# Early-solve identity in fp32r, `u` kept in the masked-key tile, and a changed emission order behind the attention

## The chip, the cores and the metric

One core of one Trainium2 chip runs the whole program. The metric is the device time of one execution in microseconds (us). The profiler's span of an execution leaves out what lies around it; for the profiled execution of the kernel before, that is 1.84 us.

## The reference, cut to what matters

Three computations in a row, all float32 (some inputs are handed over as float64, and reach the kernel as pairs of 32-bit words). B = 4, H = 8, S = 768, D = 40; the two layers see 3072 tokens of 320 numbers.

```python
for t in range(S):                                   # linear attention with a state [B, H, D, D]
    y[:, :, t] = einsum('bhd,bhde->bhe', r_t, state)
    Sa = einsum('bhde,bhe->bhd', state, a_t)
    state = state * w_t[:, :, None, :] - Sa b_t^T + v_t k_t^T
x = y as [3072, 320]
h = x @ w_in;  x = (h * sigmoid(1.702 h)) @ w_out    # layer one, 2048 hidden numbers
g = x @ w_gate;  out = ((g * sigmoid(g)) * (x @ w_val)) @ w_out2    # layer two, 1536 hidden numbers
```

## The kernel before, in words

**Attention.** The sequence is cut into 12 chunks of 64 tokens. A chunk is a chain of small float32 products on PE with copies and elementwise work on DVE and ACT between them: scores (`nb`, L740; `nk`, L995), the inverse of a triangular matrix, `w` and `u` (L1067), the state `mt` (products `m_one` and `m_two`, L1098, and for early chunks L1107), and the output `y` (L1175). In the first five chunks (`EARLY`) the two halves of the inverse are joined on PE: `cross_mm` first writes an identity into the bank (L911, a 128x128 identity times a strip of 512 columns that repeats a 32-column identity, plain float32), and then adds the cross product (L917, `x`), which goes to ACT and back (L925 `join`).

**Layer one** (class Up). Six blocks `m` of 512 tokens times 16 parts `i` of the hidden size. `h_part` has 8 products L495 into the one bank `h`, then ACT silu (L503), ACT `gh` (L509), DVE `gl` (L510). Two parts later `o_part` has 8 products (L522 to L529) into the three banks of `sums`, which are three slices of one tile. After part 15 of a block the sums are evicted: L545 (ACT, bank 1), L548 (DVE, bank 0), then L555 (ACT) and L557 (DVE) on bank 2, each followed by a DMA into `x2s` from ACT's queue (L551, L559). The next block's first `o_part` waits for all of it. The weights `wo` of two parts come by four DMAs of SP (L485), into one of two tiles.

**Layer two** (class Down). Six blocks of 512 tokens times 12 parts `f`. `h_part` has 16 products (L1456), ACT silu (L1460), DVE product (L1461), ACT `gh` (L1462), DVE `gl` (L1463); `o_part` has 12 products (L1475 to L1477).

**Weights of layer two.** They arrive as float64 pairs and are converted in 351 small jobs for 45 pieces: SP load (L301), ACT mask (L307), DVE shift (L310), DVE join (L315), POOL add (L323), ACT high half (L1369), DVE low half (L1372); pieces of `gv_rest` are followed by copies between partitions (`wg` from `wg`, L1387, SP). `prepare(n, f)` issues the next `n` jobs in that fixed order, and more if part `f` still needs some. In layer one `prepare(11)` is called behind each `gl` of the dense tasks that are left once the attention has been issued (26 times); in layer two, block 0, `prepare(f=f)` ahead of each `h_part` and `prepare(8)` twice a part. `load_x` and `split_x` (L1430 to L1441) bring the next block's tokens.

**What sets the order.** In parts one and two a planner (class Plan) takes tasks with a cost, a due time, what they read and write, and the PSUM bank pair they need (three pairs: two `ps`, and the first two banks of `sums`), and writes each engine's order. Where it finds PE without work for too long it puts in placeholder products of zeros (`h<-still`, L453, function `warm`). Behind the attention's last task the dense tasks that are left (`tail`) are issued in program order by a loop in the main function. Engines run their own streams in order.

## Time and profile before

| | us |
| --- | --- |
| median of three timed runs | 1116.86 (1115.95 to 1124.56) |
| the profiled execution | 1112.34 |
| its span in the profile | 1110.5 |
| PE busy in the span | 1073.1 (97%) |
| DVE, ACT, POOL busy | 702.2, 436.0, 98.2 |
| first product of layer one | 125.5 |
| last `x2s` DMA of layer one issued, layer two alone behind it | 712.0 |

Read it as three stages. Up to 125.5 us there is attention only, with placeholders between its products. From there to about 592 us the planner interleaves attention and layer one; from 592 to 709 us layer one runs alone on PE while the weights of layer two are converted beside it; then comes layer two.

### The profile page before, as it was taken

How to read it: one execution, taken by the hardware profiler on the slowest of the kernel's cores; microseconds unless marked ns; L12 is line 12 of the kernel's file. 1: busy time of each engine (PE TensorE's matmuls, PEld its weight loads, DVE VectorE, ACT ScalarE, POOL GpSimd, SP SyncE). 2: the span in 40 equal slices, each digit the busy share in tenths (PEclk: the TensorE clock that was granted, in tenths of full speed). 3: DMA queues.
4: the chain of work that ended last, by engine and by line, in shares of the span. 5: the costliest groups of instructions: out<-in, count | busy, mean ns of one | idle time of the engine just before them, and what ended most of it. 6: DMA issues, size and time to landing. Idle time of an engine off the chain costs nothing.

```text
span 1110.5 us, 38519 instructions
## 1 busy us (share of the span) xinstructions
PE 1073.1 (97%) x16682; PEld 892.6 (80%) x16682; DVE 702.2 (63%) x1406; ACT 436.0 (39%) x814; POOL 98.2 (9%) x115
## 2 busy tenths in 40 slices
PE   8999999899999999999999999999999999999987
PEld 7777777678778787888788878888888888888876
DVE  8976797989697887979653667643443343443221
ACT  3443646454343534344343656432222222222221
POOL 0131123320100000000000323210000000000000
PEclk9896999999999999999999999999999999999999
DMA  6265547664353543544224677430423434341000
GB/s 209 73 184 171 180 150 219 180 195 140 113 166 111 161 133 103 162 127 137 87 62 131 201 212 228 142 90 1 141 69 115 124 116 126 96 147 59 24 1 27
DMA packets 141011, 141.88 MB, mean 128 GB/s; under 512 B 16032, under 2 KB 131744, under 8 KB 140832
## 3 DMA queue, kind: packets, MB, share of 16 engines
q1 hardware_dynamic: 134784, 131.48, 39.1%
q10 hardware_dynamic: 6048, 7.86, 2.1%
q8 instruction: 132, 2.16, 0.8%
q14 instruction: 47, 0.39, 0.1%
HBM read 118.04 MB, written 13.11 MB: 118 GB/s over the span
## 4 chain that ended last, share of the span: by engine, by line
PE 87%; DVE 5%; issue 3%; DMA 2%; ACT 1%; SPq 1%; ACTq 0%; POOL 0%; DVEq 0%
PE gv L1456 24%; PE h L495 15%; PE sums L527 4%; PE oacc L1477 4%; PE oacc L1476 4%; PE oacc L1475 4%; PE sums L528 3%; PE sums L529 3%; PE h L453 3%; PE ps L1175 2%; PE sums L523 2%; PE ps L1098 2%; PE sums L522 2%; PE ps L1227 2%; PE ps L740 1%
## 5 line engine op out<-in xcount | busy, mean ns | idle before, releaser
L1456 PE MATMUL gv<-xst,wg 128*128 128x512 f32 x1152 | 279.9, 395 | 0.0
L1456 PEld LDWEIGHTS gv<-xst,wg 128*128 128x128 f32 x1152 | 213.4, 188 | 45.7
L495 PE MATMUL h<-xst,wi 120*128 120x512 f32 x768 | 197.1, 398 | 0.0
L1461 DVE TENSOR_TENSOR sg<-gv,sg 128x512 f32<-128x512 f32 x72 | 49.8, 692 | 186.5 <-PE gv L1456 184.4
L495 PEld LDWEIGHTS h<-xst,wi 120*128 120x128 f32 x768 | 140.5, 188 | 30.6
L503 ACT ACTIVATE sg<-h 128x512 f32<-128x512 f32 x96 | 57.2, 596 | 152.6 <-PE h L495 145.0
L1462 ACT ACTIVATE gh<-sg 128x512 fp32r<-128x512 f32 x72 | 45.5, 632 | 143.0 <-DVE sg L1461 143.0
L510 DVE TENSOR_TENSOR gl<-sg,gh 128x512 fp32r<-128x512 f32 x90 | 63.4, 704 | 60.2 <-ACT gh L509 60.0
L1460 ACT ACTIVATE sg<-gv 128x512 f32<-128x512 f32 x72 | 43.0, 597 | 136.6 <-PE gv L1456 136.6
L323 POOL TENSOR_TENSOR cvw<-cvu,cva 128x256 uint32<-128x256 uint32 (+2 forms) x89 | 71.6, 805 | 274.1 <-DVE cvu L315 168.5
L1476 PE MATMUL oacc<-wo,gh 128*128 128x320 f32 x288 | 89.0, 309 | 0.0
L1477 PE MATMUL oacc<-wo,gl 128*128 128x320 f32 x288 | 89.0, 309 | 0.0
L1475 PE MATMUL oacc<-wo,gh 128*128 128x320 f32 x288 | 89.0, 309 | 0.0
L527 PE MATMUL sums<-gh,wo 128*128 128x512 f32 x192 | 80.8, 421 | 2.9 <-DVE sg L557 2.6
L1463 DVE TENSOR_TENSOR gl<-sg,gh 128x512 fp32r<-128x512 f32 x72 | 49.9, 692 | 50.2 <-ACT gh L1462 50.2
L528 PE MATMUL sums<-gh,wo 128*128 128x512 f32 x192 | 75.5, 393 | 0.0
L529 PE MATMUL sums<-gl,wo 128*128 128x512 f32 x192 | 75.2, 392 | 0.0
L509 ACT ACTIVATE gh<-sg 128x512 fp32r<-128x512 f32 x96 | 60.7, 632 | 3.6 <-ACT sg L503 0.3
L788 DVE TENSOR_TENSOR tsol<-tsol,tmp 128x126 f32<-128x126 f32 (+22 forms) x217 | 56.3, 260 | 6.7
L780 DVE TENSOR_TENSOR tmp<-tsol,nsol 128x126 f32<-128x126 f32 (+22 forms) x217 | 55.8, 257 | 6.9
L453 PE MATMUL h<-still 128*128 128x512 f32 x183 | 58.3, 466 | 1.1 <-DVE still L412 1.1
L1476 PEld LDWEIGHTS oacc<-wo,gh 128*128 128x128 f32 x288 | 54.1, 188 | 3.2
(182 smaller groups left out, 1618.8 us busy)
## 6 DMA issues: line engine op xcount, KB each, us to landing
wo<-w_out SPq DMA_DIRECT2D x192, 160.0 KB
cva<-out SPq DMA_DIRECT2D x128, 128.0 KB
cva<-gv SPq DMA_DIRECT2D x96, 128.0 KB
kb<-kba SPq DMA_DIRECT2D x92, 104.0 KB
cva<-in_ab SPq DMA_DIRECT2D x64, 120.0 KB
r<-rT SPq DMA_DIRECT2D x48, 104.0 KB
vt<-vT SPq DMA_DIRECT2D x48, 104.0 KB
a<-kba SPq DMA_DIRECT2D x46, 104.0 KB
```

Source lines behind the costliest of these rows:

```text
L323: nc.gpsimd.tensor_tensor(w.bitcast(U32), u, lo, op=ALU.add)
L453: self.nc.tensor.matmul(self.ph[0], c.to_broadcast([128, 128]), c.to_broadcast([128, 512]), start=True, stop=True)
L495: nc.tensor.matmul(ps[:, 0:n], self.wi[:, b, 128 * f:128 * f + 128], x[:, a], start=(e == 0), stop=(e == 7))
L509: add("ACT", 0.63, lambda: nc.scalar.activation(out=hi, in_=sg, func=ACTF.Copy), (f"sg{s}",), (f"gh{d}",))
L510: add(("DVE", "POOL"), (0.74, 1.35), lambda e: self.engine(e).tensor_tensor(lo, sg, hi.bitcast(F32), op=ALU.subtract), (f"sg{s}", f"gh{d}" ...
L527: nc.tensor.matmul(acc[k], w[:, c:c + 128], hi, start=st, stop=False)
L528: nc.tensor.matmul(acc[k], w[:, 256 + c:384 + c], hi, start=False, stop=False)
L529: nc.tensor.matmul(acc[k], w[:, c:c + 128], lo, start=False, stop=sp)
L1456: nc.tensor.matmul(ps, w[:, b], x[:, a], start=(i == 0), stop=(i == 7))
L1475: nc.tensor.matmul(acc[k], hi[:, c], self.wo[:, f, 0], start=st, stop=False)
L1476: nc.tensor.matmul(acc[k], hi[:, c], self.wo[:, f, 1], start=False, stop=False)
L1477: nc.tensor.matmul(acc[k], lo[:, c], self.wo[:, f, 0], start=False, stop=sp)
```

## The change

1. The identity strip of `cross_mm` comes from a new fp32r tile `ones`, filled by two POOL copies at the start, and the planner's numbers for that task are lowered (cost 2.7 to 1.8, work 2900 to 2600, size 261 to 259, real 2.5 to 1.6).
2. The tile `u` is gone: `u` is written into `nk`. So the next chunk's `nk` products come behind the products that read `u`.
3. `sums` has two banks and the third is a tile of its own, `third`. The first two banks are both evicted by ACT, the third by DVE in two steps, and the three `x2s` DMAs stand behind all of them.
4. In the tail, SP's tasks and the `x2s` DMAs are held back to just behind the next `gl` (and behind its `prepare`); `prepare(11)` is left out where an eviction stands before the next `gl`; `load_x(0)` comes 28 PE tasks before the end instead of 14.

```diff
-        self.sums = q.tile([128, 3, 512], F32, name="sums")
-        self.acc = [self.sums[:, i] for i in range(3)]
+        self.sums = q.tile([128, 2, 512], F32, name="sums")
+        self.acc = [self.sums[:, 0], self.sums[:, 1], q.tile([128, 512], F32, name="third")]
...
+            first = len(plan.tasks)
+            moves = []
             for k in range(2):
                 s = sg_slot()
                 t = self.sg[s]
-                if k:
-                    add("ACT", 0.6, lambda t=t: nc.scalar.activation(out=t, in_=acc[1], func=ACTF.Copy, scale=1 / 1.702),
-                        ("acc",), (f"sg{s}",))
-                else:
-                    add("DVE", 0.7, lambda t=t: nc.vector.tensor_scalar(
-                        out=t, in0=acc[0], scalar1=1 / 1.702, scalar2=None, op0=ALU.mult), ("acc",), (f"sg{s}",),
-                        port=False)
-                add("ACT", 0.4, lambda t=t, k=k: nc.scalar.dma_start(out=xs[128 * k:128 * k + 128], in_=t),
-                    (f"sg{s}",), (), kb=256)
+                add("ACT", 0.6, lambda t=t, k=k: nc.scalar.activation(out=t, in_=acc[k], func=ACTF.Copy, scale=1 / 1.702),
+                    ("acc",), (f"sg{s}",))
+                moves.append((xs[128 * k:128 * k + 128], t, s, 256))
             s = sg_slot()
             t = self.sg[s][0:64]
-            add("ACT", 0.6, lambda: nc.scalar.activation(out=t, in_=acc[2][64:128], func=ACTF.Copy, scale=1 / 1.702),
-                ("acc",), (f"sg{s}",))
+            add("DVE", 0.65, lambda: nc.vector.tensor_scalar(
+                out=t, in0=acc[2][64:128], scalar1=1 / 1.702, scalar2=None, op0=ALU.mult), ("acc",), (f"sg{s}",),
+                port=False)
             add("DVE", 0.72, lambda: nc.vector.scalar_tensor_tensor(
                 out=t, in0=acc[2][0:64], scalar=1 / 1.702, in1=t, op0=ALU.mult, op1=ALU.add), ("acc",), (f"sg{s}",), port=False)
-            add("ACT", 0.5, lambda: nc.scalar.dma_start(out=xs[256:320], in_=t), (f"sg{s}",), (), kb=128)
+            moves.append((xs[256:320], t, s, 128))
+            for o, t, s, kb in moves:
+                add("ACT", 0.4, lambda o=o, t=t: nc.scalar.dma_start(out=o, in_=t), (f"sg{s}",), (), kb=kb)
+            for t0 in plan.tasks[first:]:
+                t0.out = True
...
-        self.i32 = cst[:, C_I:C_I + 32]
+        self.ones = one.tile([128, 160], F32R, name="ones")
...
-        self.u = one.tile([128, 16, T], F32, name="u")
+        self.u = self.nk
...
-        nc.gpsimd.memset(self.u, 0.0)
+        nc.gpsimd.memset(self.nk, 0.0)
...
+        nc.gpsimd.tensor_copy(self.ones[:, 0:128], self.ident)
+        nc.gpsimd.tensor_copy(self.ones[:, 128:160], cst[:, C_I:C_I + 32])
...
-                    ps[:, 0], self.ident, self.i32.unsqueeze(1).to_broadcast([128, 16, 32]), start=True, stop=False,
+                    ps[:, 0], self.ones[:, 0:128], self.ones[:, 128:160].unsqueeze(1).to_broadcast([128, 16, 32]), start=True, stop=False,
...
-            plan.add("PE", 2.7, cross_mm, ("xa", "dd"), ("x.p",), due + 0.1, bank=bx, into=("q0", "q1"), work=2900,
-                     size=261, real=2.5)
+            plan.add("PE", 1.8, cross_mm, ("xa", "dd"), ("x.p",), due + 0.1, bank=bx, into=("q0", "q1"), work=2600,
+                     size=259, real=1.6)
...
-        middle = plan.add("PE", 1.25, u_mm, ("w",) + tt, ("u.p",), due + 0.01, bank=bu, into=("u",))
-        plan.add(("ACT",), (0.74,), u_out, ("u.p",), ("u",), due + 0.01, bank=bu)
+        middle = plan.add("PE", 1.25, u_mm, ("w",) + tt, ("u.p",), due + 0.01, bank=bu, into=("nk",))
+        plan.add(("ACT",), (0.74,), u_out, ("u.p",), ("nk",), due + 0.01, bank=bu)
...
-            plan.add("PE", 1.25, m_two, ("u", "tok1"), ("m.p",), due + 0.02, bank=bm, work=2200)
+            plan.add("PE", 1.25, m_two, ("nk", "tok1"), ("m.p",), due + 0.02, bank=bm, work=2200)
...
-        plan.add("PE", 0.9, ut_mm, ("u",), ("ut.p",), due + 0.03, bank=bx, into=("ut",))
+        plan.add("PE", 0.9, ut_mm, ("nk",), ("ut.p",), due + 0.03, bank=bx, into=("ut",))
...
-                    parts = iter(())
-                    for t in tail:
+                    parts, later = iter(()), []
+                    for i, t in enumerate(tail):
+                        if t.eng == "SP" or hasattr(t, "out") and t.kb:
+                            later.append(t)
+                            continue
                         if t.eng == "PE":
                             if left == 2:
                                 down.begin()
                             left -= 1
                         t.run()
                         if hasattr(t, "last"):
-                            down.prepare(11)
+                            ends = [hasattr(x, "last") for x in tail[i + 1:]] + [True]
+                            if not any(hasattr(x, "out") for x in tail[i + 1:i + 1 + ends.index(True)]):
+                                down.prepare(11)
+                            for x in later:
+                                x.run()
+                            later = []
                         if t.eng == "PE":
-                            if left == 14:
+                            if left == 28:
                                 down.load_x(0)
                             elif left == 10:
                                 parts = down.split_x(0)
                             next(parts, None)
+                    for x in later:
+                        x.run()
```

**PE, 15th part of layer one, fifth chunk.** Before: L522 and L495 are dense products, L965 is `t_mm`, L453 the placeholder, L740 the next chunk's scores.

```order
L522 MATMUL sums<-gh_100,wo_106 128x512
L495 MATMUL h<-xst_93,wi 128x512 x8
L965 MATMUL ps_123<-q,tn 32x32 x32
L453 MATMUL h<-still 128x512 x4
L740 MATMUL ps_122<-kb,a_126 32x32 x4
L740 MATMUL ps_122<-kb,a_126 32x64 x4
L740 MATMUL ps_122<-kb,a_126 32x32 x4
```

After (three lines further down in the file; L1051 is `w_two`, L1070 `u_mm`):

```order
L959 MATMUL ps_124<-tt,nb_141 32x32 x32
L495 MATMUL h<-xst_93,wi 128x512 x8
L1039 MATMUL ps_123<-v,nk 64x40 x32
L968 MATMUL ps_124<-q,tn 32x32 x32
L453 MATMUL h<-still 128x512
L1051 MATMUL ps_123<-mt,a_127 64x40 x32
L453 MATMUL h<-still 128x512 x7
L1070 MATMUL ps_124<-w,tt 64x40 x32
L1110 MATMUL ps_123<-mt,cst 104x320 x2
```

The scores of the next chunk (L740, L743 after) no longer stand ahead of `u_mm`, and one and seven placeholders stand there instead of four; five more follow behind L1085 of the same chunk. In all there are 194 placeholders instead of 183: 178 ahead of the first product of layer one before and 176 after, 5 behind it before and 18 after.

**ACT, the boundary between blocks 4 and 5 of layer one.** Before: L545 and L555 evict, L551 and L559 send, L503 and L509 belong to the first parts of block 5, L307 and L1369 are conversions.

```order
L1369 ACTIVATE wo_10357<-cvw_79 128x256
L307 ACTIVATE cva_76<-cva_76 128x256
L1369 ACTIVATE wg<-cvw_80 128x2x128
L545 ACTIVATE sg_98<-sums 128x512
L551 DMA x2s<-sg_98 128x512
L555 ACTIVATE sg_95<-sums 64x512
L551 DMA x2s<-sg_97 128x512
L503 ACTIVATE sg_96<-h 128x512
L509 ACTIVATE gh_100<-sg_96 128x512
L559 DMA x2s<-sg_95 64x512
L307 ACTIVATE cva_77<-cva_77 128x256
L1369 ACTIVATE wg<-cvw_79 128x2x128
```

After (L546 evicts, L558 sends, L1372 is the former L1369):

```order
L503 ACTIVATE sg_96<-h 128x512
L509 ACTIVATE gh_99<-sg_96 128x512
L546 ACTIVATE sg_97<-sums 128x512
L546 ACTIVATE sg_98<-sums 128x512
L503 ACTIVATE sg_96<-h 128x512
L509 ACTIVATE gh_100<-sg_96 128x512
L1372 ACTIVATE wg<-cvw_80 128x2x128
L307 ACTIVATE cva_77<-cva_77 128x256
L1372 ACTIVATE wg<-cvw_79 64x2x128
L558 DMA x2s<-sg_97 128x512
L558 DMA x2s<-sg_98 128x512
L558 DMA x2s<-sg_95 64x512
```

Both evictions stand together, no conversion stands ahead of them and none between `L509` and them, and the DMAs come behind the next part's L503 and L509 and three conversions.

**DVE, layer two, block 0, part 9 into part 10.** Before: L1461 and L1463 are the product and `gl` of a part, L1438 and L1441 split the next block's tokens.

```order
L1461 TENSOR_TENSOR sg_96<-gv,sg_96 128x512
L1463 TENSOR_TENSOR gl_102<-sg_96,gh_99 128x512
L1438 TENSOR_TENSOR xst_94<-xr,xst_94 128x512
L1461 TENSOR_TENSOR sg_97<-gv,sg_97 128x512
L1463 TENSOR_TENSOR gl_103<-sg_97,gh_100 128x512
L1441 SCALAR_TENSOR_TENSOR xst_94<-xst_94,cst,xr 128x512
```

After (L1464, L1466, L1441 and L1444 are the former L1461, L1463, L1438 and L1441, L1375 the former L1372):

```order
L1466 TENSOR_TENSOR gl_102<-sg_96,gh_99 128x512
L1441 TENSOR_TENSOR xst_94<-xr,xst_94 128x512
L1375 TENSOR_TENSOR wg<-cvw_79,wg 128x2x128
L310 TENSOR_SCALAR cvu_81<-cva_78 128x256
L315 SCALAR_TENSOR_TENSOR cvu_81<-cva_78,cvu_81 128x256
L1375 TENSOR_TENSOR wg<-cvw_80,wg 128x2x128
L310 TENSOR_SCALAR cvu_82<-cva_76 128x256
L315 SCALAR_TENSOR_TENSOR cvu_82<-cva_76,cvu_82 128x256
L1375 TENSOR_TENSOR wg<-cvw_79,wg 64x2x128 x2
L310 TENSOR_SCALAR cvu_81<-cva_77 128x256
L315 SCALAR_TENSOR_TENSOR cvu_81<-cva_77,cvu_81 128x256
L1375 TENSOR_TENSOR wo_10539<-cvw_80,wo_10539 128x256
```

Conversions now stand between part 9 and part 10, among them the last piece of `gv_rest` (L1375 on 64 partitions, twice). Before, the last conversion of all stood behind the `gl` of part 3. In the tail of layer one `prepare(11)` now runs 16 times (176 jobs) instead of 26 (286): the attention's last product stands behind part 75 of layer one and not part 67, and two calls are left out. So 175 jobs and not 65 are left to block 0 of layer two.

## Rows read from the trace of the kernel before

**Rows 1.** The page, the chain that ended last, share by engine.
```profile
PE 87%; DVE 5%; issue 3%; DMA 2%; ACT 1%; SPq 1%; ACTq 0%; POOL 0%; DVEq 0%
```
**Rows 2.** Windows: length, busy per engine PE PEld DVE ACT POOL, granted PE clock, DMA.
```profile
0.00:125.50 125.50, 113.40 (x3084) 91.35 (x3084) 101.44 (x166) 49.83 (x102) 21.00 (x32) 0.88 0.52 157
44.00:52.00 8.00, 7.85 (x167) 6.38 (x167) 7.42 (x19) 4.07 (x9) 0.66 (x1) 0.62 0.12 33
80.00:100.00 20.00, 17.56 (x472) 13.27 (x466) 12.21 (x27) 8.42 (x18) 2.94 (x4) 0.66 0.77 238
...
652.00:656.00 4.00, 4.00 (x18) 3.29 (x19) 2.86 (x6) 1.63 (x5) 1.10 (x2) 1.00 0.94 313
```
**Rows 3.** Timeline of PE, first chunk's solve: start, duration, line, count.
```profile
30.93 1.02 PE L911 MATMUL ps<-cst 128*128 128x512 f32 x2
32.03 1.25 PE L917 MATMUL ps<-nsol,tsol 32*16 32x32 f32 x128
33.21 2.45 PE L453 MATMUL h<-still 128*128 128x512 f32 x10
```
**Rows 4.** PE's waits, one group: total, times, longest (us).
```profile
PE sums L527 <- DVE sg L557: 2.6, 1, 2.6
```
**Rows 5.** Timeline around the boundary of blocks 4 and 5; in brackets the idle time before.
```profile
647.38 2.00 PE L495 MATMUL h<-xst,wi 120*128 120x512 f32 x8
...
649.25 0.58 ACT L545 ACTIVATE sg<-sums 128x512 f32<-128x512 f32 x1
...
649.86 0.69 DVE L548 TENSOR_SCALAR sg<-sums 128x512 f32<-128x512 f32 x1
...
651.21 0.68 DVE L557 SCALAR_TENSOR_TENSOR sg<-sums,sg 64x512 f32<-64x512 f32 x1 [0.66 <-ACT sg L555]
...
651.94 0.50 PE L527 MATMUL sums<-gh,wo 128*128 128x512 f32 x1 [2.56 <-DVE sg L557]
```
**Rows 6.** The same timeline at the boundary of layer one and layer two.
```profile
709.92 0.69 DVE L548 TENSOR_SCALAR sg<-sums 128x512 f32<-128x512 f32 x1 [2.12 <-ACT sg L545]
```
**Rows 7.** Timeline, layer two, block 0, parts 9 and 10 of before, PE and DVE.
```profile
751.23 3.89 PE L1456 MATMUL gv<-xst,wg 128*128 128x512 f32 x16
...
756.72 3.66 PE L1456 MATMUL gv<-xst,wg 128*128 128x512 f32 x15
...
756.62 0.69 DVE L1463 TENSOR_TENSOR gl<-sg,gh 128x512 fp32r<-128x512 f32 x1 [0.70 <-ACT gh L1462]
757.23 0.68 DVE L1438 TENSOR_TENSOR xst<-xr,xst 128x512 fp32r<-128x512 f32 x1
```
**Rows 8.** Timeline of the last conversions of before, each engine's step.
```profile
722.76 0.41 ACT L1369 ACTIVATE wg<-cvw 128x256 fp32r<-128x256 f32 x1
...
723.18 0.29 DVE L310 TENSOR_SCALAR cvu<-cva 128x256 uint32<-128x256 uint32 x1
723.50 0.42 DVE L315 SCALAR_TENSOR_TENSOR cvu<-cva,cvu 128x256 uint32<-128x256 uint32 x1
723.84 0.42 DVE L1372 TENSOR_TENSOR wg<-cvw,wg 128x256 fp32r<-128x256 f32 x1
...
724.14 0.75 POOL L323 TENSOR_TENSOR cvw<-cvu,cva 128x256 uint32<-128x256 uint32 x1 [2.36 <-DVE cvu L315]
...
728.70 2.72 SPq L1387 DMA_DIRECT2D wg<-wg  x4
```
**Rows 9.** Timeline, a small copy's issue on two queues and the work that waited for it.
```profile
593.51 2.28 SPq L1255 DMA_DIRECT2D xm<-su  x3
...
595.91 0.81 ACTq L1255 DMA_DIRECT2D xm<-su  x1
597.74 0.42 ACT L1262 ACTIVATE xst<-xm 120x256 fp32r<-120x256 f32 x1 [2.04 <-DMA xm<-su]
```
**Rows 10.** Timeline of SP's queue behind a part of layer one: loads for conversion, loads of `wo`.
```profile
645.19 2.90 SPq L301 DMA_DIRECT2D cva<-gv  x6
...
651.34 1.94 SPq L485 DMA_DIRECT2D wo<-w_out  x4
```

## The prediction

> **What bounds the kernel now.** I read the chain that ended last first: PE holds 87% of it [rows 1], and of 1110.5 us of span PE is busy 1073. So a microsecond counts if PE issues less, waits less, or runs at a higher clock; work on another engine counts only where PE waits for it. The windows come next. They show the one stretch where the clock is not full: 0.88 on average up to 125.5 us, with 0.62 at 44 to 52 and 0.66 at 80 to 100 [rows 2]. At a mean of 0.88 the stretch loses 0.12 x 125.5 = 15 us of full-speed time; the two dips hold 0.38 x 8 = 3.0 and 0.34 x 20 = 6.8 of it. Then PE's waits: with dense work there is a single long one, 2.6 us for an eviction [rows 4]. Last, the timelines at the three places that the change touches.
>
> **Identity.** The two records of L911 (the plain float32 product runs as two) start at 30.93 and L917 follows at 32.03 [rows 3]: a slot of 1.10 us, with PE waiting for nothing between. In the new type it is one pass of 512 columns. The trace has no 128x512 fp32r identity, but its dense products are of that type and width: 16 take 3.89 us and step by (756.72 - 751.23 - 12 x 0.147) / 16 = 0.233 [rows 7], so one alone lasts 3.89 - 15 x 0.233 = 0.40; with 0.08 for the change of type behind the drain I take 0.48 (my choice). That is -0.62 in each of five chunks, **-3.1**. Lower bound 0, if the cross product then waits for DVE anyway; upper bound -0.9 each where the clock is at half and the slot longer, -4.4.
>
> **Placeholders.** Eleven more, nearly all behind the first dense product. Ten take 2.45 us, a step of 0.24 [rows 3]: **+2.6** if PE had no gap there; 0 if they fill gaps that PE has anyway. I take the first, since from 125.5 on PE has next to no gap.
>
> **u in nk.** The order changes in the first chunk alone, where `nk_mm` of the next chunk goes behind `u`'s readers; in the later chunks it stood there already. It has placeholders on both sides there, which are the cover: 0. Without that cover, the scores of one chunk, 1.2 us, would move onto the chain.
>
> **Eviction.** Before, each of the four steps waits for the one before, on the other engine: 649.25, 649.86, 651.21 at the start of three of them, end 651.89, and PE resumes at 651.94 after 2.56 us [rows 5]. After, ACT does 0.58 + 0.6 while DVE does about 0.65 + 0.68, 1.35 us, and no conversion stands ahead of them on ACT. The block's last sum is issued just ahead of the eight products at 647.38, which take 2.00 [rows 5], so 1.35 is covered: **-2.56, +0.3** for what comes late behind (the silu of the fourth part waits for the `x2s` DMA that now stands behind three conversions; 0 to 2). What makes the four steps serial is the tile and not the bank: L548 stood idle 2.12 us until L545 was done, though it reads another bank [rows 6]. The Trainium skill, PSUM — Partial Sum Buffer, in its table of terms, says that two engines collide only on the same bank and the same quarter of the partitions; by that rule alone L548 could have run beside L545 before, and the split would be worth nothing. The trace speaks against that reading, so the split counts.
>
> **Conversions pushed into layer two.** This is the largest term. 176 jobs and not 286 are done in the tail, 175 are left at 16 a part, so by part 10 of block 0 336 are issued and 349 are wanted: 13 go directly ahead of `h_part(0,10)`, with the last `gv_rest` piece among them. Let t0 be the end of `h_part(0,9)`, 754.96 in before's time. `gl` is done at 757.31 (t0 + 2.35), the token split on DVE at 757.91 (+2.95) [rows 7]. Behind them on DVE: a low half 0.42, shift 0.29, join 0.42, with 0.03 between, at +4.1; POOL 0.75, +4.85; ACT 0.41, +5.3; issue of the copy 2.72 / 4 = 0.68, +5.95 [rows 8]; and its landing. For that I have an xst that waited for small copies: the last of SP's three is issued by 595.79, the one on ACT's queue by 596.72, and the work starts at 597.74 [rows 9], so 1.0 or 1.95 us. So the third product of part 10, which reads that piece, can go at +7.0 to +7.9. It is wanted at 12 x 0.147 + 2 x 0.233 = +2.23. The stall is 4.7 to 5.7; with up to 0.35 of backlog on DVE from the part before I take **+5.5** (0 if the pieces are ready, 8 if SP's queue is occupied). Queued behind it: PE's part 10 alone, and block 1 is not late for anything else. The other 160 jobs lie beside products: a part lasts 5.49 us on PE (756.72 - 751.23), and about two pieces ask DVE for 2 x (0.29 + 0.42 + 0.42) = 2.3 beside its own 2 x 0.69 + 0.68 = 2.1.
>
> **wo loads.** They are now issued behind one more part's `gl` and its conversion loads. A part of layer one is 16 x 0.23 = 3.68. From `gl` of one part (R): 3.68, six loads 2.9, one issue 1.94 / 4 = 0.49 [rows 10], landing 1.95: R + 9.0; the product that reads it stands five half parts on, R + 5 x 1.84 = 9.2. So it is just in time or, with a partition copy or a buffer wait in SP's queue, late by 0.3 to 0.8. In four pairs of parts: **+1.5** (0 to 5).
>
> **Early clock.** The order ahead of layer one has the same products, with more placeholders before the scores of chunk 2 (13, was 7) and before the solve's end in chunks 3 and 4, just ahead of the two dips. I give back a fifth of their 9.8 us: **-2** (from -10, both gone, to +7, a third dip of the size of the larger).
>
> **Sum.** -3.1 + 2.6 + 0 - 2.56 + 0.3 + 5.5 + 1.5 - 2 = +2.2 on 1112.34, so 1114.6 for an execution like the profiled one. The median of the timed runs is 4.5 above the profiled execution, so against 1116.86 this is **1119**.
>
> **Rivals.**
> *A, conversions keep up.* If the jobs run ahead of the order that I count (part 10 has no stall) and `wo` is in time, the sum is -3.1 + 2.6 - 2.3 - 2 = -4.8: 1112. For it: DVE is idle for most of layer two's parts in before. Against: the engines run in order, and the rows in DVE's stream stand behind part 9's `gl`.
> *B, the other side: the clock stays up.* If the order ahead of layer one keeps PE's clock full, the 15 us of the first stretch come back whole in place of 2: 1119 - 13 = 1106, and 1100 with A. It decides if both dips are gone, not one. For it: the dips follow stretches with little on PE, and the placeholders are denser now. Against: the number ahead of layer one hardly changes (178 and 176).
> *C, the gap costs the clock.* PE idles over 5 us in part 10, more than anywhere with dense work in before; the gap of 2.56 left the clock at 1.00 [rows 2]. If it falls for as long as at 44 to 52 us, another 3.0 us are lost, if as at 80 to 100, 6.8: 1122 to 1126. The Trainium skill, TensorE: Matmul & The Clock Gate, section HAM oscillation, says that idle gaps between bursts of products bring the clock to half and that each burst behind one starts cold. By that rule the gap in part 10 costs its stall and a cold start; the trace shows dips only in the first 125 us, and no gap of this length.
> *D, late wo at every pair.* If each of some ten pairs of the tail is late by 1 us and not four by 0.4, 8.5 more: 1128. It decides from 1.1 us a pair on.
> *E, the identity does nothing,* as DVE ends the chain there: +3.1, 1122.
>
> **How the numbers follow.** My case 0.45 (1115 to 1123 with its own bounds), A 0.22, B 0.08, C 0.12, D 0.08, E 0.05. A measurement of this kernel can tell about 1% from no change (11.2 us). Only B is below 1105.7, only the upper ends of C and D reach past 1128: faster 0.09, same 0.83, slower 0.08. The range leaves most of B and D out: 1108 to 1127.
>
> **What would show it.** In the profile of the changed kernel: one record of the identity of 0.4 to 0.5 us and L917 right behind; ACT's two evictions and DVE's two side by side, and PE's wait for them gone; a wait of about 5 us on PE at the third product of part 10 of layer two's first block, released by a copy `wg` from `wg`; short waits of PE for `wo` in the tail; the clock at 0.6 to 0.7 again in two places before the first dense product. Wrong would be: no wait in part 10 (A), a mean clock near 1.00 in the first stretch (B), a clock under 1.00 behind part 10 (C), or PE waiting for `wo` in most parts (D).

## The result, and the profile after

The changed kernel takes 1131.66 us in the median of six runs (1127.83 to 1136.7); the kernel before, run in turn with it, 1118.78 (1115.95 to 1124.56). The ratio is 1.0127, interval 1.0096 to 1.0158: slower by 13 us in the medians and 14 by the ratio, where the prediction had 1119 as the likeliest, 1108 to 1127 as its range and 0.08 for slower. A second set on another chip gives 1.0112 (1.0072 to 1.0151).

The profiled execution of the changed kernel took 1127.83 us, its span 1126.0, 15.5 more than that of the kernel before. The page shows less PE work and more waiting around it; in the chain PE has fallen from 87% [rows 1] to 78%, and DMA has risen from 2% to 5%:

```profile
PE 1072.2 (95%) x16688; PEld 890.9 (79%) x16688; DVE 699.9 (62%) x1400; ACT 435.0 (39%) x814; POOL 101.0 (9%) x123
...
PE 78%; DVE 7%; DMA 5%; issue 4%; SPq 2%; ACT 2%; POOL 0%; ACTq 0%; DVEq 0%; POOLq 0%
```

PE's waits by group (total, times, longest, in us) name what is new. The wait for the eviction [rows 4] is gone; one for the partition copy `wg` from `wg`, some for `wo`, and one for a silu stand instead:

```profile
PE gv L1459 <- DMA wg<-wg: 7.3, 1, 7.3
...
PE sums L527 <- DMA wo<-w_out: 2.3, 3, 1.4
...
PE h L495 <- ACT sg L503: 0.9, 1, 0.9
```

The windows, with the columns of [rows 2], show the first stretch at a granted clock of 0.99 (1.00 is full speed) in this execution, where it was 0.88, and half speed at another place, in part 10 of layer two's first block:

```profile
0.00:114.30 114.30, 100.59 (x3080) 82.74 (x3080) 98.30 (x160) 48.71 (x100) 22.76 (x32) 0.99 0.56 170
...
763.60:768.20 4.60, 0.61 (x3) 0.17 (x2) 3.87 (x9) 2.86 (x7) 1.02 (x2) 1.00 0.25 69
768.20:775.10 6.90, 3.60 (x9) 2.85 (x10) 3.48 (x8) 2.28 (x5) 2.12 (x3) 0.51 0.45 127
```

**Part 10.** PE's timeline (start, duration, line, count, idle time before) has its first two products, the wait, and the start of part 11:

```profile
763.58 0.63 PE L1459 MATMUL gv<-xst,wg 128*128 128x512 f32 x2
771.50 4.88 PE L1459 MATMUL gv<-xst,wg 128*128 128x512 f32 x13 [7.29 <-DMA wg<-wg]
...
778.21 1.33 PE L1459 MATMUL gv<-xst,wg 128*128 128x512 f32 x5
```

Part 10 takes 778.21 - 763.58 = 14.63 us where a part takes 5.49 [rows 7]: **9.1 us** more, of which 7.3 are the wait; the rest goes with the clock, 0.51 in the window from 768.2 on, in which PE works for 3.6 us. DVE, POOL and SP in the same stretch show why the copy is late:

```profile
760.83 0.74 POOL L323 TENSOR_TENSOR cvw<-cvu,cva 128x256 uint32<-128x256 uint32 x1 [3.02 <-DVE cvu L315]
...
760.87 0.86 DVE L310 TENSOR_SCALAR cvu<-cva 128x256 uint32<-128x256 uint32 x1
...
762.44 0.87 DVE L310 TENSOR_SCALAR cvu<-cva 128x256 uint32<-128x256 uint32 x1
...
763.69 0.68 DVE L1464 TENSOR_TENSOR sg<-gv,sg 128x512 f32<-128x512 f32 x1
...
765.07 0.69 DVE L1466 TENSOR_TENSOR gl<-sg,gh 128x512 fp32r<-128x512 f32 x1 [0.70 <-ACT gh L1465]
...
769.33 2.65 SPq L1390 DMA_DIRECT2D wg<-wg  x4
```

Measured from the end of part 9's products (761.82, counted as the prediction counted t0), the product L1464 starts at +1.87 where before it started at +0.27 (755.23 - 754.96), since conversions stand ahead of it on DVE; `gl` ends at +3.94 and not at +2.35, the copy is issued at +7.5, and PE resumes at +9.7 where it wanted +2.2. A shift L310 takes 0.86 and not 0.29 [rows 8] when it starts beside POOL's L323, and two pieces of a burst stand 762.44 - 760.87 = 1.57 us apart.

**The boundary of blocks 4 and 5.** The rows of ACT, DVE, ACT's queue, SP and PE that answer to [rows 5]:

```profile
650.86 1.08 ACT L546 ACTIVATE sg<-sums 128x512 f32<-128x512 f32 x2 [0.35 <-PE sums L529]
...
651.34 0.69 DVE L551 TENSOR_SCALAR sg<-third 64x512 f32<-64x512 f32 x1
...
652.07 0.68 DVE L554 SCALAR_TENSOR_TENSOR sg<-third,sg 64x512 f32<-64x512 f32 x1
...
653.61 0.50 PE L528 MATMUL sums<-gh,wo 128*128 128x512 f32 x1 [0.18 <-DMA wo<-w_out]
...
653.67 0.84 ACTq L558 DMA_DIRECT2D x2s<-sg  x2
...
659.41 0.60 ACT L503 ACTIVATE sg<-h 128x512 f32<-128x512 f32 x1 [4.28 <-DMA x2s<-sg]
...
659.58 2.18 SPq L485 DMA_DIRECT2D wo<-w_out  x4
...
660.06 2.11 PE L495 MATMUL h<-xst,wi 120*128 120x512 f32 x8 [0.89 <-ACT sg L503]
```

The eviction takes 652.75 - 650.86 = 1.9 us on two engines side by side, and the next `o_part` waits only for `wo`. But two things come late behind it. The `sg` tile that the first `x2s` DMA sends is the one that the silu at 659.41 writes next: that DMA is issued at 653.67 and lands at 659.33, ACT waits 4.28 us for it, and PE 0.89 us for the silu. And SP issues the next `wo` at 659.58, because its queue stood behind `load_x(0)`, which the change brought forward to this place. The view of the chain that ended last, from 648 to 664 us (start, us, what):

```profile
651.96 6.07 DMA xr<-x2s
...
658.09 0.68 SPq L1390
...
659.58 3.17 DMA wo<-w_out
...
662.80 0.50 PE sums L527
```

L1390 copies `wg` and doesn't read `xr`; in the trace it counts on the same semaphore as the first load of `load_x(0)`, and so waits for its landing. The three `x2s` DMAs beside that load take 5.5 to 7.3 us from issue to landing. Before, where `load_x(0)` was issued 29 us behind them, they took 2.0 to 3.9.

From the first product of part 84 (the parts of layer one counted from 1 to 96) to layer two the changed kernel needs 708.58 - 655.33 = 53.25 us, the kernel before 701.73 - 653.90 = 47.83, **5.4 us** less (these four are starts of rows of PE's timeline, of after and of before):

```profile
655.33 0.86 PE L495 MATMUL h<-xst,wi 120*128 120x512 f32 x3
...
708.58 0.62 PE L1459 MATMUL gv<-xst,wg 128*128 128x512 f32 x2
```
```profile
653.90 0.85 PE L495 MATMUL h<-xst,wi 120*128 120x512 f32 x3
...
701.73 0.62 PE L1456 MATMUL gv<-xst,wg 128*128 128x512 f32 x2
```

At 655.33 the changed kernel is 1.4 us late, at layer two 6.9, behind part 10 16.0. So the profiled difference is 1.4 up to and with the eviction, 5.4 in the tail and 9.1 in part 10. A part without a wait takes 3.68 us here; by the lengths of the parts from 84 on, 1.1 of the 5.4 go with the silu and 4.3 with late `wo`, the largest 1.2 in part 85 (662.80) and 1.9 in part 95.

**Ahead of the eviction.** The 1.4 hide a gain and a loss. The first product of layer one comes 125.5 - 114.3 = 11.2 us earlier in this execution, but part 83 starts 650.88 - 647.38 = 3.5 later. Windows from the first product of layer one to the attention's last, after and before:

```profile
114.30:625.10 510.80, 490.65 (x11246) 398.52 (x11241) 374.15 (x797) 222.37 (x395) 43.76 (x46) 0.99 0.45 136
```
```profile
125.50:592.10 466.60, 453.51 (x11105) 368.23 (x11102) 369.76 (x789) 211.69 (x376) 43.28 (x39) 1.00 0.47 142
```

PE is idle there for 20.2 us and not 13.1, and the clock is at half in three places, 13.6 us in sum.

### The profile page after: what moved, and what is told of

Same layout as the page of the kernel before. It is cut to its first block, busy times and chain, and to the rows that moved or that the text cites. A ratio compares the mean times of both kernels' runs of the same rounds, so it can differ in the third digit from the quotient of the medians.

```text
span 1126.0 us, 38515 instructions
## 1 busy us (share of the span) xinstructions
PE 1072.2 (95%) x16688; PEld 890.9 (79%) x16688; DVE 699.9 (62%) x1400; ACT 435.0 (39%) x814; POOL 101.0 (9%) x123
## 4 chain that ended last, share of the span: by engine, by line
PE 78%; DVE 7%; DMA 5%; issue 4%; SPq 2%; ACT 2%; POOL 0%; ACTq 0%; DVEq 0%; POOLq 0%
PE gv L1459 21%; PE h L495 14%; PE sums L527 4%; PE sums L528 3%; PE sums L529 3%; PE oacc L1480 3%; PE oacc L1478 3%; PE oacc L1479 3%; PE ps L1230 2%; PE third L523 2%; PE ps L1178 2%; PE third L522 2%; PE ps L1101 2%; DMA wo<-w_out 1%; PE h L453 1%
## 5 line engine op out<-in xcount | busy, mean ns | idle before, releaser
L495 PE MATMUL h<-xst,wi 120*128 120x512 f32 x768 | 197.4, 399 | 0.9 <-ACT sg L503 0.9
L495 PEld LDWEIGHTS h<-xst,wi 120*128 120x128 f32 x768 | 140.3, 188 | 32.0 <-ACT sg L503 1.5
L1464 DVE TENSOR_TENSOR sg<-gv,sg 128x512 f32<-128x512 f32 x72 | 49.8, 692 | 177.8 <-PE gv L1459 176.4
L503 ACT ACTIVATE sg<-h 128x512 f32<-128x512 f32 x96 | 57.2, 596 | 156.4 <-PE h L495 133.2
L323 POOL TENSOR_TENSOR cvw<-cvu,cva 128x256 uint32<-128x256 uint32 (+2 forms) x89 | 74.4, 836 | 272.3 <-DVE cvu L315 154.3
L1463 ACT ACTIVATE sg<-gv 128x512 f32<-128x512 f32 x72 | 42.9, 595 | 132.5 <-PE gv L1459 132.5
L527 PE MATMUL sums<-gh,wo 128*128 128x512 f32 x192 | 82.1, 428 | 2.3 <-DMA wo<-w_out 2.3
L1466 DVE TENSOR_TENSOR gl<-sg,gh 128x512 fp32r<-128x512 f32 x72 | 49.8, 692 | 50.2 <-ACT gh L1465 50.2
L528 PE MATMUL sums<-gh,wo 128*128 128x512 f32 x192 | 77.2, 402 | 0.2 <-DMA wo<-w_out 0.2
L509 ACT ACTIVATE gh<-sg 128x512 fp32r<-128x512 f32 x96 | 60.7, 632 | 3.3
L1479 PEld LDWEIGHTS oacc<-wo,gh 128*128 128x128 f32 x288 | 54.1, 188 | 3.2
L1478 PEld LDWEIGHTS oacc<-wo,gh 128*128 128x128 f32 x288 | 54.1, 188 | 3.1
```

Source lines behind the costliest of these rows:

```text
L323: nc.gpsimd.tensor_tensor(w.bitcast(U32), u, lo, op=ALU.add)
L495: nc.tensor.matmul(ps[:, 0:n], self.wi[:, b, 128 * f:128 * f + 128], x[:, a], start=(e == 0), stop=(e == 7))
L503: nc.scalar.activation(out=sg, in_=state["h"][:, 0:n], func=ACTF.Silu, scale=1.702)
L509: add("ACT", 0.63, lambda: nc.scalar.activation(out=hi, in_=sg, func=ACTF.Copy), (f"sg{s}",), (f"gh{d}",))
L527: nc.tensor.matmul(acc[k], w[:, c:c + 128], hi, start=st, stop=False)
L528: nc.tensor.matmul(acc[k], w[:, 256 + c:384 + c], hi, start=False, stop=False)
```

## The experiments

All ratios are to the kernel before, run in turn on the same chip. Executions of one kernel differ by some 1% here, so for each run the span is also split: the clock's part is the span times one minus its mean granted clock, the rest is what remains. Both, in us, as differences of means from the kernel before of the same chip:

| run | ratio (interval) | clock's part | rest |
| --- | --- | --- | --- |
| e1_ident_u | 1.0104 (1.0061 to 1.0147) | +1.4 | +6.5 |
| e2_eviction | 0.9996 (0.9963 to 1.0029) | +2.6 | -3.0 |
| e3_more_jobs | 1.0152 (1.0085 to 1.022) | +8.0 | +7.8 |
| e4_sp_in_place | 1.0121 (1.0075 to 1.0168) | +6.2 | +4.5 |
| e5_u_alone | 1.0037 (1.0007 to 1.0066) | +1.4 | +2.5 |
| e6_u_identity_old_numbers | 1.0088 (1.0055 to 1.0122) | +8.6 | -0.1 |
| e7_ten_jobs | 1.0105 (1.0066 to 1.0144) | -1.9 | +12.0 |
| e8_numbers_float32 | 0.9999 (0.9969 to 1.0028) | -4.2 | +5.4 |
| e9_identity_twice | 1.0043 (1.0008 to 1.0078) | +3.9 | +1.8 |
| e10_more_placeholders | 1.0066 (1.003 to 1.0103) | -1.5 | +9.5 |
| e11_changed_float32 | 1.011 (1.0076 to 1.0145) | +1.7 | +10.2 |
| e12_best_guess | 0.9977 (0.9943 to 1.001) | -2.4 | +0.5 |
| e13_changed_again | 1.0112 (1.0072 to 1.0151) | +3.0 | +9.1 |
| e14_ident_u_again | 1.0049 (1.002 to 1.0078) | -1.3 | +6.9 |
| e15_numbers_float32_again | 1.0041 (1.0006 to 1.0077) | -1.9 | +6.6 |
| e16_old_tail | 1.0009 (0.9975 to 1.0044) | +1.8 | +0.3 |

The differences in the clock's part have standard errors of 1.2 to 2.6 us, those in the rest of 0.8 to 1.8 (e3 2.6), so differences of the clock's part below 4 us say little.

**Parts alone.** The first two put the change's attention edits and its eviction, each alone, on the kernel before; their diffs are the hunks shown with the change, from `i32` to `ut_mm` for e1, and from `sums` to `t0.out` for e2.

> Alone on the kernel before: the fp32r identity with its planner numbers, and u in nk (the identity tile fits only where u is gone). Eviction and tail stay as before. Theory 'order': these two edits alone make the attention's new order, with its 16 placeholders behind the first dense product, so PE reaches the last dozen parts of layer one 3 to 6 us later than before, although the first dense product comes 3 to 6 us earlier; time +3 to +6 us, ratio 1.003 to 1.006. Rival 'identity saves': the identity's 3 us come through to the end, time -2 to -5 us. Rival 'tail': what the changed kernel lost up to the last parts of layer one came from its eviction, then this run is level with before or faster at that point.

> Alone on the kernel before: the third bank as a tile of its own, two evictions on ACT and two steps on DVE, the x2s DMAs behind them; identity, u and the tail's emission as before. Theory: PE's wait of 2.56 us at the boundary of blocks 4 and 5 is gone, with at most 1 us given back to a silu that waits for an x2s DMA; nothing moves in block 0 of layer two. Time -1.5 to -2.5 us, ratio 0.9975 to 0.999. Rival 'sg is late': the silu and wo after the boundary give it all back, 0 to +1 us.

e1 is slower by 8 us in the mean (and the same kernel, e14, by 6), with 6.5 to 6.9 us in the rest. That is the way of theory 'order' and more than its 3 to 6: e1's first product of layer one comes 6.4 us earlier than before, and its part 84 starts at 665.83, 11.9 later. Both rivals fall. e2 is level: 3.0 us less in the rest, somewhat more than its theory said, offset by 2.6 in the clock's part, which has an error of 1.9. In its profile PE still waits 1.2 us for L546 at the boundary, where it had waited 2.56.

**Part 10 and the tail.** e3 changes one number and takes the condition away, e4 leaves SP's tasks where they were, e7 changes the two calls of a part.

```diff
-    if not any(hasattr(x, "out") for x in tail[i + 1:i + 1 + ends.index(True)]):
-        down.prepare(11)
+    down.prepare(14)                                                  # e3
...
-    if t.eng == "SP" or hasattr(t, "out") and t.kb:
+    if hasattr(t, "out") and t.kb:                                    # e4
...
-                self.prepare(8)
+                self.prepare(10)                                      # e7, both calls
```

> The changed kernel with 14 jobs behind each of the 18 gl of the tail and no call left out (252 jobs instead of 176), the order of SP's tasks as changed. Theory: the wait of 7.3 us in part 10 of layer two's first block and the half-speed clock behind it vanish, 9.1 us less than the changed kernel; the tail stays 3.4 us behind. Time against before 1.004 to 1.008. Rival 'moved into the tail': the 76 jobs more make wo and the halves in the tail later, and 3 to 6 of the 9 us come back there: 1.008 to 1.012.

> The changed kernel with SP's tasks (the wo loads) issued in their place in the tail, only the x2s DMAs still held back; the left-out conversions stay left out. Theory: PE's waits for wo in the tail go (about 4 us of the changed kernel's loss between the eviction and the end of layer one), the wait in part 10 stays at 7.3 us: 3 to 5 us less than the changed kernel, 1.008 to 1.010 of before. Rival 'conversions were held up instead': wo in its place makes the loads for conversion late and part 10 waits longer, no gain.

> The changed kernel with 10 jobs at each of the two calls of a part in layer two's first block instead of 8, so that the last piece that part 10 needs is converted one part earlier; tail and attention as changed. Theory: the wait of 7.3 us at the third product of part 10 and the slow clock behind it go, and nothing comes back, as the parts have room on DVE: 9 us less than the changed kernel. Rival 'moved': the halves of each part now wait behind conversions and PE waits a little in several parts, 3 to 6 us come back.

In e3 the wait in part 10 is gone altogether, so it is the number of jobs left that makes it. But its rival holds, and goes further than it said: PE's waits from 640 us on, in the view by group, are now those of the tail, and its ratio, 1.0152, is the highest of all (its interval takes in the changed kernel's):

```profile
PE sums L527 <- DMA wo<-w_out: 5.3, 4, 1.9
PE h L495 <- ACT sg L503: 3.9, 1, 3.9
PE sums L528 <- DMA wo<-w_out: 0.9, 1, 0.9
```

In e4 no wait for `wo` is left and that of part 10 stays, as its theory said, and so does the silu's; the rest is 4.5 where e13 has 9.1, but the clock's part takes most of that back, and its ratio shows no gain. e4 still has `load_x(0)` 28 tasks ahead; no run moves that load alone. e7 refutes its theory: with ten jobs a call PE still waits twice for the copy, 3.0 us in sum, and twice for L1463, whose turn on ACT is behind conversions. Layer two takes 417.8 us in its profile and 417.5 in the changed kernel's, so nothing is gained. The parts don't have the room that the prediction's sum gave them: with a shift at 0.86 two pieces ask DVE for 2 x (0.86 + 0.42 + 0.42) = 3.4 us, and with the part's own 2.1 that is all of the 5.49 (an estimate from these durations).

```profile
PE gv L1459 <- DMA wg<-wg: 3.0, 2, 2.2
...
PE gv L1459 <- ACT sg L1463: 1.3, 2, 0.8
```

**The identity.** Three pairs differ in its product alone, with the same order of PE: e6 and e5, e1 and e8, the changed kernel and e11. e9 issues the product twice.

```diff
-            plan.add("PE", 1.8, cross_mm, ("xa", "dd"), ("x.p",), due + 0.1, bank=bx, into=("q0", "q1"), work=2600,
-                     size=259, real=1.6)
+            plan.add("PE", 2.7, cross_mm, ("xa", "dd"), ("x.p",), due + 0.1, bank=bx, into=("q0", "q1"), work=2900,
+                     size=261, real=2.5)                              # e6, on e1
...
+                for _ in range(2):                                    # e9, on e6: the product of `ones` twice
...
-                    ps[:, 0], self.ones[:, 0:128], self.ones[:, 128:160].unsqueeze(1).to_broadcast([128, 16, 32]), start=True, stop=False,
+                    ps[:, 0], self.ident, self.i32.unsqueeze(1).to_broadcast([128, 16, 32]), start=True, stop=False,   # e8 on e1, e11 on the change
```

> Alone on the kernel before: u written into nk; the identity in plain float32 with its old planner numbers, eviction and tail as before. The order has 190 placeholders, 185 ahead of the first dense product and 5 behind (183, 178 and 5 before). Theory 'numbers': the loss of the first experiment comes from the identity's new planner numbers, which put 16 placeholders and the waits of PE behind the first dense product; then u alone is level with before but for the first chunks, 0 to +3 us, and PE's idle time from the first dense product to the attention's end stays at 13 to 15 us. Rival 'u': the reuse of the tile itself makes the chain wait, +7 to +11 us and 18 to 20 us of idle time there.

> The same as e5_u_alone, and the identity's product in fp32r while the planner keeps its old numbers: PE's order is that of e5_u_alone row for row. So the pair prices the product alone. Theory: five slots go from 1.10 to about 0.46 us and all of it comes through, -3 us against e5_u_alone, and the first dense product comes 2 to 3 us earlier. Rival 'DVE ends the chain there': the time goes into a wait ahead of the cross product, and the two are level. Against the first experiment, which differs in the planner's numbers alone, theory 'numbers' expects this one 6 to 10 us faster.

> u in nk and the identity's new planner numbers, but its product in plain float32: PE's order is that of the first experiment row for row, the product alone differs. It is the second pair for the product's price. Split each run's span into the part that the clock took (span times one minus the mean granted clock) and the rest. Theory 'clock': as in the pair of the second batch (2.6 us less in the rest, 7 us more for the clock with fp32r), this one has 2 to 3 us more in the rest than e1_ident_u and 3 to 7 us less for the clock: level with it or up to 4 us faster. Rival 'chance': the clock's part does not depend on the product, and this one is 3 us slower than e1_ident_u.

> e6_u_identity_old_numbers with each of the five fp32r identities issued twice (the second overwrites the first), so PE is as busy there as with plain float32. Theory 'clock': the part that the clock takes falls back from 26 us to that of e5_u_alone, 19 us, and the rest rises by 1 to 1.5 us: 4 to 6 us faster than e6_u_identity_old_numbers, level with e5_u_alone. Rival 'chance': the clock's part stays near 26 us and the time is 1 us above e6_u_identity_old_numbers.

> The changed kernel with one thing undone: the identity's product is plain float32 again. Planner numbers, u in nk, eviction and tail stay, and with them PE's order and its 194 placeholders. Theory 'clock': as in the pairs e6/e5 and e1/e8, the part that the clock takes falls by 5 to 7 us and the rest moves by -1 to +3: 3 to 9 us less than the changed kernel, 1.005 to 1.010 of the kernel before, with the wait of 7.3 us in part 10 unchanged. Rival 'identity saves': 3 us more, 1.015.

e5 is 3.9 us slower than before in the mean, just above theory 'numbers' and far below 'u', but PE's idle time from the first product of layer one to the attention's end is 485.80 - 466.86 = 18.9 us in its profile (window 127.0 to 612.8), as 'u' said. So putting `u` into `nk` is not free by itself. e6 is level with e1 rather than 6 to 10 us faster, so 'numbers' doesn't hold for the time either; in the rest alone it does (-0.1 and +6.5).

e6 is 5 us slower than e5, with 2.6 less in the rest and 7 more in the clock's part, and e9 lies between. That, and e8 against e1, looked as if PE, less busy with the shorter identity, lost its clock more often. e8 and e1 had run on different chips, though, and e11, with 1.011, does not differ from the changed kernel. So the partners were put on one chip, with the changed kernel, and with its tail as before:

> The changed kernel itself, on the chip of the next three, so that it can be set against them in time and in the part that the clock takes. Both theories: 1.011 to 1.014 of the kernel before.

> The kernel of e1_ident_u, beside its partner with the float32 identity on one chip. Theory 'clock': fp32r costs 3 to 8 us against the partner, all of it in the part that the clock takes. Rival 'chance': 1 to 3 us faster than the partner.

> The kernel of e8_numbers_float32, the partner of the one before: same order of PE, identity in plain float32. Theory 'clock': 1.000 to 1.003 of the kernel before. Rival 'chance': 1.005 to 1.010.

> The changed kernel with the tail emitted as before (11 jobs behind every gl, wo loads and x2s DMAs in their places, load_x 14 tasks ahead); identity, numbers, u and eviction as changed. Theory: no wait in part 10 and no late wo, 9 + 3 us less than the changed kernel, 1.001 to 1.005 of the kernel before. Rival 'moved': the attention ends later than before, so the old tail too is short of calls (some 200 jobs of 351), and part 10 waits again.

e14 and e15 are level in time, in the rest and in the clock's part (0.7 us apart, error 2.0). So neither theory 'clock', which wanted 3 to 8 us, nor its rival's saving is borne out for this order. It is not refuted in general: e6 and e5, the other pair on one chip, are 7.2 apart in the clock's part (error 3.0) and were not repeated, and in none of the pairs, e16 and e12 among them (1.0009 and 0.9977, on two chips), has the fp32r kernel the lower ratio. Whether the shorter product costs clock stays open; that it saves 3 us at the end is not seen. PE's timeline of e14 shows the product as short as the prediction had it (33.49 - 33.01 = 0.48 us to the cross product, and 30.82 - 29.72 = 1.10 in e15, as in [rows 3]); the 3 us of five such slots are too little to see beside what changes from run to run.

```profile
33.01 0.40 PE L913 MATMUL ps<-ones 128*128 128x512 f32 x1
33.49 0.70 PE L919 MATMUL ps<-nsol,tsol 32*16 32x32 f32 x64
```

e16 decides the rest. The changed kernel with the old tail is level with the kernel before, and e13, which differs in the tail's emission alone (point 4 of the change, all of it), is 10.1 us slower in the mean, with an error of 2.0, or by the ratios 1.0112 / 1.0009 = 1.0103, 11.5 us: the new emission costs **10 to 11.5 us** of the 12 that separate e13 from the kernel before. Its profile has these waits of PE from 640 to 800 us:

```profile
PE h L495 <- ACT sg L503: 1.7, 1, 1.7
PE gv L1459 <- DMA wg<-wg: 0.6, 1, 0.6
PE third L522 <- DVE sg L554: 0.6, 1, 0.6
```

The wait in part 10 is 0.6 us and not 7.2 as in e13, and none is for `wo`. The count of jobs fits: the old tail calls `prepare(11)` behind all its 18 `gl`, 198 jobs and not 176, so by part 10, at 16 a part, 358 are issued where the prediction counted 336, and 349 are wanted. Its rows of PE for part 84 and for layer two's start are at 662.46 and 712.28, 49.8 us apart and not 53.25. So 3.4 in the tail, and 9.1 less the 0.9 by which e16's part 10 is still longer, are 11.6, near both figures. (To the end of the span the two profiles differ by 8.5 from part 84 on, as e16's clock is at half for 6.8 us more at 1092 us.)

```profile
662.46 0.89 PE L495 MATMUL h<-xst,wi 120*128 120x512 f32 x3
...
712.28 1.09 PE L1459 MATMUL gv<-xst,wg 128*128 128x512 f32 x4
```

**Versions that might beat both.** e12 is e8 with the eviction of e2; e10 is e2 with one number of the planner changed:

```diff
-    WINDOW, KEEP, DENSITY, WIDE, STILL = 3.4, 4000.0, 1600.0, 5000.0, 640.0
+    WINDOW, KEEP, DENSITY, WIDE, STILL = 3.4, 4500.0, 1600.0, 5000.0, 640.0
```

> A version that may beat both: the kernel before with the new eviction alone (as e2_eviction), and the planner's activity target raised from 4000 to 4500, which puts in 216 placeholders and not 183 (189 ahead of the first dense product, 27 behind it). Theory: 33 placeholders cost up to 8 us at 0.24 each, less where PE idles anyway, and the clock's part falls from 17 to 20 us to 8 to 12: 2 to 6 us less than the kernel before. Rival 'cost': the clock's part hardly moves and the time rises by 4 to 8 us.

> The version that may beat both: u in nk and the new planner numbers with the identity in plain float32 (e8_numbers_float32, 0.9999), and the new eviction (e2_eviction, 0.9996), with the tail emitted as before. If the two add up: 3 us less outside the clock than e8, ratio 0.996 to 1.000 of the kernel before. If the silu behind the boundary waits for the x2s DMA as in e2: level with it.

e10 has 9.5 us more in the rest than the kernel before and 1.5 less in the clock's part; against e2, which lacks only its 33 placeholders and ran on another chip, that is 12.5 more and 4.1 less. So rival 'cost' holds. e12 has the lowest ratio of all, but its interval holds 1: no version here is shown to be faster than the kernel before.

## Why the prediction was wrong

The step that failed is the price of the tail's new emission. The prediction gave +7.3 for it (5.5 for part 10, 1.5 for `wo`, 0.3 for the silu); the profile shows 14.5 (9.1 and 5.4), and undoing the emission alone brings 10 to 11.5 us back (e16).

**Conversions pushed into layer two: the mechanism was right, the size was not.** The wait came at the third product of part 10, released by the copy it named. It was put at 5.5 and measured 7.3, and with the clock behind it 9.1. Two terms failed. "Up to 0.35 of backlog on DVE" was 1.6: the shift was priced at 0.29 [rows 8], as it runs alone, and takes 0.86 beside POOL's L323, so a burst advances a piece in 1.57 us and not 1.13. Two shifts of 0.57 more make 1.1 of the 1.6. The Trainium skill, SBUF — State Buffer, section SBUF: two separate sides, says that GpSimd and DVE work in a two-port mode or with two SBUF inputs share one port pair, which whichever starts first holds for its whole instruction while the other blocks. The trace agrees: a shift that starts 0.04 us behind POOL's 0.74 ends 0.16 us behind it; that the shift runs in such a mode is not shown. And the clock's fall was a rival (C, 0.12), not a part of the sum: a gap of 2.56 us had left it at 1.00 [rows 2], one of 7.3 brought it to 0.51 for 6.9 us.

**wo loads and the silu behind the eviction: two small terms, both too small.** "+1.5" measured 4.3 and "+0.3" measured 1.1, from part 84 on. Both lie inside the bounds given (0 to 5, 0 to 2), and were taken near their low ends. The earlier `load_x(0)` had no term at all, though SP's queue and the `x2s` DMAs stand behind or beside it at the boundary. e16 keeps 2.0 of the 5.4, and none of it is for `wo` or an `x2s` DMA: there a silu stands on ACT behind a mask whose `cva` load, issued behind `load_x(0)` at its old place, is late.

```profile
695.96 0.43 ACT L307 ACTIVATE cva<-cva 128x256 uint32<-128x256 uint32 x1 [3.31 <-DMA cva<-gv]
...
697.44 1.43 PE L495 MATMUL h<-xst,wi 120*128 120x512 f32 x5 [1.67 <-ACT sg L503]
```

The 3.4 of the held-back tasks and the earlier load are what rival D was about, at less than half of its 8.5; how they divide was not measured.

**The eviction: right.** PE's wait of 2.56 us [rows 5] is gone, and from part 83 to part 84 the profile gives 2.1 us back (655.33 - 650.88 = 4.45 for 653.90 - 647.38 = 6.52). Alone (e2) it takes 3.0 us out of the rest, which doesn't show in the ratio.

**Identity: right in the slot, wrong in the sum.** 0.48 us was the slot. -3.1 shows in the rest of one pair (e6 against e5, -2.6, error 1.8) and in the time of none. What the planner made of the edits counts for more: e1, e8, e14 and e15 have 5.4 to 6.9 us more in the rest, e5 2.5, where the prediction had 2.6 for placeholders and nothing for `u`. It reasoned that from 125.5 us on "PE has next to no gap"; in the kernel before, PE is idle there for 13.1 us up to the attention's end, and in the changed kernel's profile for 20.2. Its four terms ahead of the eviction add up to -2.5, and in the profiled execution part 83 starts 3.5 later. With the eviction and the old tail (e12, e16) the excess in the rest is down to 0.3 to 0.5. Which of the order's waits make it, and why they shrink when the planner sees the other eviction too, was not taken apart.

**Early clock: luck, and not a term.** "-2" was read from the order of placeholders. The changed kernel's profile does have its first stretch at 0.99. But e13, the same kernel, has 0.94 up to its first product of layer one at 119.5, and e3, with the same order there, has 0.88 again, as the kernel before had:

```profile
0.00:126.50 126.50, 110.99 (x3080) 90.17 (x3080) 98.39 (x160) 48.52 (x100) 23.22 (x33) 0.88 0.52 154
```

It changes from execution to execution, so rival B happened in the profiled run and brought nothing to the median; nor did it help that run, which had lost the 11.2 us again by part 83.

**The range.** The base was one execution at the low end of its kernel: 1112.34, 6.4 below the median of six. The terms for the tail were taken near their low ends, and C and D stood as alternatives to the main case, though each could only come on top of it. With 9.1 for part 10, and 5.4 - 2.1 in place of -0.8 for eviction and tail, its own sum is +9.9: 1122 for an execution like the profiled one, and with the 4.5 or 6.4 between that and the median, 1127 to 1129. That is 3 to 6 us short of 1127.83 and 1131.66, and the terms ahead of the eviction were off by 6.0.

## What to carry to other kernels

Before calls that convert ahead are left out or moved, count what is left at the deadline. Price it as a burst on in-order engines, with the durations that the steps have beside each other, and let the late wait pull the clock down in the same sum. Here 22 jobs, two calls of `prepare(11)`, lie between a wait of 0.6 us (e16) and one of 7.2 (e13). A load that is brought forward needs a term too: for what is queued behind it, and for what is in flight beside it. A short wait that is removed is worth less than its length where the tiles, loads and DMAs that it used to cover are moved behind it. A clock that dips in one execution is a property of that execution until a second one of the same order shows it too.

## What the runs showed of the hardware

The granted clock of the first 125 us differs between executions of the same order of instructions: 0.99 in the changed kernel's profile, 0.88 in e3's, with 12 us between them at the first product of layer one. The shift L310 on DVE takes 0.29 us alone and 0.86 when it starts just behind POOL's L323. And two eviction copies on ACT run back to back in 1.08 us while DVE reads the third bank, where the kernel before, with all three banks in one tile, had each wait for the other engine [rows 6].
